# Groups of 768 tokens: twelve second products in hand, softmax transposes on 96 partitions in place, separate accounts for VectorE and ScalarE

## The chip, the cores and the metric

The kernel runs on one core of a Trainium2 chip. What counts is the device time of one execution in microseconds (us). TensorE does the matrix products, VectorE, ScalarE and GpSimd the elementwise work, and SyncE (SP) issues the DMAs. In rows of the trace the engines are PE (PEld for its weight loads), DVE, ACT, POOL and SP. Each engine runs its own instructions in order and waits on semaphores of the others.

## What is computed

```python
# 8 batches, 8 heads, 576 tokens, head size 64; heads 0-3 plain window of 32, heads 4-7 dilated by 4
scores = scale * q @ k^T, masked to the window
attn   = exp(scores - max) / (sum + 1e-9)
x      = (attn @ v), 8 heads side by side      # 4608 tokens x 512
h = x @ w_in                                   # 512 -> 2048
g = where(h > 0, h, exp(min(h, 0)) - 1)        # ELU
out = g @ w_out                                # 2048 -> 512
```

## The kernel before

**Split operands.** A 32-bit operand is kept as a high part and a rest, and a product is made of three: high by high, rest by high, high by rest. Making the parts is one ScalarE copy (a *cast*) and one VectorE subtraction (a *rest*) each.

**Chunks and groups.** The first 1536 tokens go through the two layers as three chunks of 512 (loop over `c` in `range(CS)`, line 913, 16 blocks `f` of 128 hidden columns each). The other 3072 tokens go as four groups of 768 (`superchunk`, line 773), each of two halves of 384 tokens. In a group the first layer is done by seven block products in place of eight: a *round* (`q`, 8 a group) makes two blocks of hidden columns for both halves, in seven *steps* (`s`, 0 to 6; `ORDER`, `MOVING`). A step is six matmuls of 128x384 (`product`, line 708; rows `h<-...`).

**A round's elementwise work** (`TODO`, line 54). The products accumulate in two PSUM tiles, x (steps 0, 1, 2, 5) and y (3, 4, 6). ScalarE copies x out after steps 0, 1 and 2 (`u1`, `u2`, `u3`; rows `e<-h`) and after step 5 (`C21`; row `a-1<-h`). VectorE adds y to one of the copies after steps 3, 4 and 6 (`C11`, `C22`, `C12`; rows `a-1<-h,e`). So step 1 waits for `u1`, step 2 for `u2`, step 4 for `C11`, step 6 for `C22`, and the next round's step 0 for `C21`. Then the ELU: `exp`, `relu` on ScalarE into one scratch tile `e` (rows `a<-...` 128x768), `elu` on VectorE. Block 1 (the odd one) comes from `C21` and `C22`, block 0 from `C11` and `C12`. A trailing `<` means the previous round's block. Last, `cast` and `rest` split the first half's 384 tokens into a *set* (`gh`, `gl`), and `keep` writes the second half's to DRAM (`aside`). After the eight rounds a loop over 16 blocks brings these back (`bring`), casts them and makes the operands of the next group (`OPERANDS`, `moving_operand`).

**Second products in hand.** A finished block is queued as three second products, one for each 128 tokens, of three 128x512 matmuls each (`push`, line 730; rows `o_ps<-...`). Step 5 queues block 1 and step 6 block 0, before their casts have run. `pop` takes products from the front of that queue (`fifo`), `POPS` says how many after each step: two after steps 0, 1 and 3. The first round uses `FIRST_POPS`. A finished output tile is copied by ScalarE and stored (`store`, line 608).

**Attention beside it.** Attention of later batches is done two heads' pairs at a time, in eight *blocks* (`BLOCKS`): an `S` piece (144 small score matmuls, then VectorE adds the masks), softmax steps held in a list (`side`), and an `O` piece (probabilities by values). `PIECES` gives the step (7q+s) at which a piece stands. `work(spare)` (line 443), called at `w0` to `w6`, takes softmax steps from the list as long as an account of VectorE time is positive; `work_all` empties it ahead of a piece. A block's two heads' pairs take turns in a fixed order. The probabilities are transposed by VectorE straight into the zeroed tiles `pt`, six 32-partition transposes for a pair (line 474). The chunk before the first group also makes blocks of batch 3 (`WHEN`), the first later block's scores (`EARLY`) and eight weight combinations (`COMBINE`).

The order on each engine in the groups is the program's own: `vec` and `act` (line 434) keep it.

Of the kernel before, what the change touches and what calls it, by code (L numbers as in the profile page):

```python
# [23 lines left out]
P = 128  # L24
# [36 lines left out]
WHEN = {1: (0, 6, 7, 13), 2: (0, 4, 5, 9)}  # L61
EARLY = 10
# [12 lines left out]
def body(ctx: ExitStack, tc: tile.TileContext, q, k, v, masks, w_in, w_out, out):  # L75
# [359 lines left out]
    side, held, credit = [], [], [0.0]  # L435

    def work_all():

        while side:
            side.pop(0)[1]()  # L440
        credit[0] = 0.0

    def work(spare):

        credit[0] = min(credit[0] + spare, 0.0) if not side else credit[0] + spare
        while side and credit[0] > 0:
            cost, step = side.pop(0)
            step()
            credit[0] -= cost

    def later_probabilities(b, hps, groups):
# [9 lines left out]
        def steps(j):  # L461

            sm, (mx, sums), tr = sms[j], small[j], trs[j]
            yield 0.9, lambda: vec.tensor_reduce(out=mx, in_=sm, op=ALU.max, axis=mybir.AxisListType.X)
            yield 0.9, lambda: vec.tensor_tensor(out=sm, in0=sm, in1=wide(mx), op=ALU.subtract)
            yield 0.0, lambda: act.activation(out=sm, in_=sm, func=AF.Exp, scale=0.125)
            yield 0.9, lambda: vec.tensor_reduce(out=sums, in_=sm, op=ALU.add, axis=mybir.AxisListType.X)
            yield 0.1, lambda: vec.tensor_scalar(out=sums, in0=sums, scalar1=1e-9, scalar2=None, op0=ALU.add)
            yield 0.1, lambda: vec.reciprocal(out=sums, in_=sums)
            yield 0.9, lambda: vec.tensor_tensor(out=sm, in0=sm, in1=wide(sums), op=ALU.mult)  # L470
# [137 lines left out]
    def store(c, t, o_ps):  # L608
        if c < CS:
# [57 lines left out]
    def more_sets():  # L667

        sets[1:1] = [tuple(fp.tile([P, TC], F32R, name=n, bufs=m)[:, :TH] for n, m in (("gh", 3), ("gl", 2))) for _ in range(2)]
        out_tiles.extend(fp.tile([P, DM], F32, name=n, bufs=m) for n, m in (("h", 2), ("h", 2), ("gh", 3)))  # L670
# [64 lines left out]
    def activation(what):  # L735
# [7 lines left out]
        if do == "exp":  # L743
# [12 lines left out]
    def piece(what):  # L756
# [16 lines left out]
    def superchunk(c):  # L773
        x_ps = y_ps = None
        for q in range(NQ):
            base = (c * NQ + q) * 7
            for s in range(7):
                load_combined(base + s + RING)
                if (c, q, s) == (0, 2, 0):
                    more_sets()  # L780
# [6 lines left out]
                for what in TODO[s]:  # L787
# [8 lines left out]
                    elif what[0] == "w":  # L796
                        work(SPARE[s])
# [19 lines left out]
        for f in range(NF):  # L817
# [11 lines left out]
            work(2.0)  # L829
# [83 lines left out]
    for c in range(CS):  # L913
# [14 lines left out]
        for f in range(NF):  # L928
# [53 lines left out]
            if c == CS - 1 and f >= EARLY:  # L982
                work(2.6)
# [80 lines left out]
```

## Time and profile before

| | us |
|---|---|
| median of 3 runs (1000.48 to 1004.38) | 1004.24 |
| the profiled execution, its own time | 1003.11 |
| its span, first to last instruction | 1001.3 |
| PE busy in it | 900.7 |
| DVE busy | 624.7 |
| ACT busy | 474.7 |

The first group begins at 347.26 us of the span, the next ones at 529.71, 686.84 and 847.29. A row of the timeline begins with start and length, and gives in brackets the engine's idle time ahead of it and what ended that.

### The profile page before, as it was taken

To read this page: it belongs to the slowest core of one execution; us is meant where nothing else is said; L and a number is where in the kernel's file an instruction comes from. 1 tells how busy PE (TensorE), PEld (TensorE's weight loads), DVE (VectorE), ACT (ScalarE), POOL (GpSimd) and SP (SyncE) were. 2 spreads that over 40 slices of the span, in tenths; PEclk is the share of its full clock that TensorE was granted. 3 is DMA by queue.
4 is the path that set the end of the run, shared out by engine and by line. 5 is a ranking of instruction groups with operands and counts; after the bars stand their busy time and mean duration, and the time that the engine had idled before them with its cause. 6 is when DMAs were issued, how large, how long until landed. Compare 5 with 4: busy or idle time off the path is not lost.

```text
span 1001.3 us, 17241 instructions
## 1 busy us (share of the span) xinstructions
PE 900.7 (90%) x6752; PEld 726.6 (73%) x6752; DVE 624.7 (62%) x1015; ACT 474.7 (47%) x913; POOL 6.0 (1%) x12
## 2 busy tenths in 40 slices
PE   6999999999898897897799888989788989888888
PEld 5446677788676676787687767878677878877766
DVE  6999989676886875747461857353566526233331
ACT  4765666465544543443453435453443444444442
POOL 2000000000000000000000000000000000000000
PEclk8999999999998997998999999999999989999999
DMA  9977352235444256755454765634754543655532
GB/s 352 382 260 248 98 159 94 81 125 200 167 156 142 56 157 186 222 166 175 124 159 150 213 191 169 192 114 121 223 161 144 175 127 87 200 167 167 157 103 79
DMA packets 93457, 166.45 MB, mean 166 GB/s; under 512 B 9696, under 2 KB 40768, under 8 KB 93376
## 3 DMA queue, kind: packets, MB, share of 16 engines
q1 hardware_dynamic: 93376, 165.36, 52.4%
q8 instruction: 53, 0.87, 0.4%
q14 instruction: 28, 0.23, 0.1%
HBM read 124.42 MB, written 40.89 MB: 165 GB/s over the span
## 4 chain that ended last, share of the span: by engine, by line
PE 59%; DVE 19%; ACT 15%; issue 4%; DMA 2%; SPq 0%; DVEq 0%; ACTq 0%
PE o_ps L112 31%; PE h L112 24%; ACT a L432 7%; DVE a-1_3348 L432 3%; PE a_ps L112 3%; DVE pt L419 2%; DVE pt L432 1%; ACT e L432 1%; DMA r<-combined 1%; DVE sums L432 1%; DVE a L432 1%; DVE r L432 1%; DVE e L584 1%; DMA out<-e 1%; ACT a-1_3348 L432 1%
## 5 line engine op out<-in xcount | busy, mean ns | idle before, releaser
L112 PE MATMUL h<-xall,r 128*128 128x384 f32 (+1 forms) x708 | 158.4, 371 | 5.7 <-DVE a-1_3348 L432 3.0
L112 PE MATMUL o_ps<-a,gh 128*128 128x512 f32 x434 | 149.3, 438 | 11.9 <-ACT gh L432 8.7
L112 PE MATMUL h<-r,r 128*128 128x384 f32 x526 | 130.5, 348 | 23.9 <-DVE a-1_3348 L432 16.2
L112 PEld LDWEIGHTS h<-xall,r 128*128 128x128 f32 x708 | 130.2, 192 | 24.7 <-DVE a-1_3348 L432 4.4
L112 PEld LDWEIGHTS h<-r,r 128*128 128x128 f32 x526 | 95.6, 193 | 35.4 <-DVE a-1_3348 L432 23.9
L112 PEld LDWEIGHTS o_ps<-a,gh 128*128 128x128 f32 x434 | 81.3, 190 | 45.0 <-issue 17.2
L432 DVE TENSOR_TENSOR a-1_3348<-h,e 128x384 f32<-128x384 f32 x96 | 53.2, 554 | 88.7 <-PE h L112 86.8
L432 ACT COPY e<-h 128x384 f32<-128x384 f32 x96 | 45.4, 473 | 128.1 <-PE h L112 126.9
L432 DVE SCALAR_TENSOR_TENSOR a-1_3348<-a-1_3348,a 128x768 f32<-128x768 f32 x64 | 61.2, 957 | 56.9 <-ACT a L432 50.6
L112 PE MATMUL h<-a,r 128*128 128x384 f32 x384 | 94.7, 340 | 0.0
L112 PE MATMUL o_ps<-r,gh 128*128 128x512 f32 x242 | 79.4, 410 | 9.6 <-ACT gh L432 8.8
L112 PE MATMUL o_ps<-a,r 128*128 128x512 f32 x288 | 77.5, 402 | 10.4 <-ACT r L432 7.5
L112 PE MATMUL o_ps<-a,gl 128*128 128x512 f32 x173 | 69.6, 402 | 6.1 <-DVE gl L588 3.7
L112 PEld LDWEIGHTS h<-a,r 128*128 128x128 f32 x384 | 70.6, 191 | 4.4
L112 PEld LDWEIGHTS o_ps<-a,r 128*128 128x128 f32 x288 | 53.1, 190 | 24.2 <-ACT r L432 9.1
L432 ACT COPY a-1_3348<-h 128x384 f32<-128x384 f32 x32 | 15.3, 479 | 110.2 <-PE h L112 106.5
L432 ACT ACTIVATE a<-a-1_3348 128x768 f32<-128x768 f32 x64 | 54.1, 846 | 21.6 <-DVE a-1_3348 L432 20.6
L432 ACT ACTIVATE a<-a 128x768 f32<-128x768 f32 (+1 forms) x72 | 60.4, 845 | 5.1 <-DVE a L432 3.2
L112 PEld LDWEIGHTS o_ps<-r,gh 128*128 128x128 f32 x242 | 46.6, 197 | 20.3 <-ACT gh L432 10.5
L432 DVE TENSOR_TENSOR r<-a-1_3348,r 128x384 fp32r<-128x384 f32 (+1 forms) x39 | 23.2, 596 | 45.9 <-ACT r L432 45.7
L112 PE MATMUL o_ps<-r,gl 128*128 128x512 f32 x117 | 48.0, 411 | 0.7 <-DVE gl L432 0.7
L112 PEld LDWEIGHTS o_ps<-a,gl 128*128 128x128 f32 x173 | 33.0, 191 | 16.4 <-DVE gl L588 5.0
(189 smaller groups left out, 1394.7 us busy)
## 6 DMA issues: line engine op xcount, KB each, us to landing
r<-combined SPq DMA_DIRECT2D x224, 256.0 KB, 3.0
aside<-a-1_3348 SPq DMA_DIRECT2D x64, 192.0 KB, 2.7
vt<-v SPq DMA_DIRECT2D x30, 384.0 KB, 3.9
kt<-k SPq DMA_DIRECT2D x30, 304.0 KB, 4.7
qt<-q SPq DMA_DIRECT2D x30, 288.0 KB, 4.2
r<-w_in SPq DMA_DIRECT2D x16, 512.0 KB, 7.1
r<-w_out SPq DMA_DIRECT2D x16, 512.0 KB, 7.8
combined<-a SPq DMA_DIRECT2D x20, 256.0 KB, 2.9
```

Source lines behind the costliest of these rows:

```text
L112: return inorder(nc.tensor.matmul(*args, **kw))
L419: last_transpose[b] = nc.vector.transpose(out=tr[ks, :, cs], in_=sm[cs, :, rs]).ins
L432: return lambda *args, **kw: inorder(getattr(self.eng, name)(*args, **kw))
L584: v.scalar_tensor_tensor(out=e, in0=h_ps, scalar=0.0, in1=e, op0=ALU.max, op1=ALU.subtract)
```

## The change

- The queue of second products is kept at twelve (an assertion at the end of each group says so): `FIRST_POPS` takes two fewer in the first round, and no piece stands any more at a step where it takes two beyond the table. Both casts and rests now stand at step 1.
- The odd block's ELU moves into its own round: its exponential is cut into two halves (`expR1` at step 4 from `C22`, `expL1` at step 5 from `C21`), `elu1` and `keep1` come after step 6.
- The probabilities are transposed in place by VectorE, two instructions on 96 partitions for a pair, and ScalarE copies six 32x384 pieces into `pt`.
- `work` has one account for VectorE and one for ScalarE, chooses the first step that is ready, and takes the two pairs of a block as they come. `work_all` empties the list only up to a given block.
- The pieces, the combinations, the attention of batch 3 and the first later block's scores move; one of the two extra sets and two output tiles come a round earlier; chunk 2's stores use them if they are there.

```diff
-FIRST_POPS = (2, 2, 1, 2, 1, 1, 1)
-TODO = [t.split() for t in ("u1 elu1< keep1< exp0< relu0< w0", "u2 elu0< keep0< cast1< rest1< w1", "u3 cast0< rest0< w2", "C11 w3", "C22 w4", "C21 exp1 relu1 w5 push1", "C12 w6 push0")]
-SPARE = (1.0, 0.6, 0.9, 1.5, 0.4, 1.3, 0.0)
+FIRST_POPS = (2, 2, 0, 2, 1, 1, 0)
+TODO = [t.split() for t in ("u1 exp0< relu0< w0", "u2 elu0< keep0< cast1< cast0< rest1< rest0< w1", "u3 w2", "C11 w3", "C22 expR1 w4", "C21 expL1 relu1 w5 push1", "C12 elu1 keep1 w6 push0")]
+SPARE = ((1.4, 0.4), (0.3, 0.9), (1.2, 1.7), (1.8, 1.7), (0.7, 0.0), (0.8, 0.0), (0.0, 0.0))
-WHEN = {1: (0, 6, 7, 13), 2: (0, 4, 5, 9)}
-EARLY = 10
+WHEN = {1: (0, 6, 7, 13), 2: (0, 6, 7, 12)}
+EARLY = 14
-PIECES = {0: {1: "S1", 7: "O0", 21: "S2", 24: "O1", 40: "S3", 44: "O2"}, 1: {8: "S4", 28: "S5", 33: "O4", 50: "O5"}, 2: {8: "S6", 28: "S7", 33: "O6", 50: "O7"}}
+PIECES = {0: {14: "S1", 17: "O0", 28: "S2", 31: "O1", 42: "S3", 45: "O2"}, 1: {7: "S4", 28: "S5", 31: "O4", 45: "O5"}, 2: {7: "S6", 28: "S7", 31: "O6", 45: "O7"}}
-COMBINE = {(1, 11): 0, (1, 13): 1, (1, 15): 2, (2, 1): 3, (2, 2): 4, (2, 4): 5, (2, 6): 6, (2, 8): 7}
+COMBINE = {(1, 11): 0, (1, 13): 1, (1, 15): 2, (2, 1): 3, (2, 4): 4, (2, 6): 5, (2, 9): 6, (2, 11): 7}
...
+    def next_step(vec_free, act_free):
+        seen = set()
+        for n, (block, pair, copies, on_act, cost, step) in enumerate(side):
+            when, where = latest.get((block, pair), (0, on_act))
+            ready = (block, pair) not in seen and (where == on_act or when < turn[0]) and not (copies and block - 1 in made)
+            seen.add((block, pair))
+            if ready and (act_free if on_act else vec_free) > 0:
+                return n
...
-            for c in range(GU):
-                for r in range(2):
-                    yield 0.57, lambda ks=ks, cs=cs, rs=rs: vec.transpose(out=tr[ks, :, cs], in_=sm[cs, :, rs])
+            for r in range(2):
+                part = sm[:, :, r * G:(r + 1) * G]
+                yield False, False, 0.57, lambda part=part: vec.transpose(out=part, in_=part)
+            for r in range(2):
+                for c in range(GU):
+                    yield True, True, 0.45, lambda ks=ks, cs=cs, rs=rs: act.copy(out=tr[ks, :, cs], in_=sm[cs, :, rs])
...
-                if (c, q, s) == (0, 2, 0):
-                    more_sets()
+                if (c, s) == (0, 0) and q in (1, 2):
+                    more_sets(q == 2)
...
-        if c < CS:
+        if not out_tiles:
             o = fp.tile([P, DM], F32, name="e")
...
-            work(2.0)
+            work(2.0, 0.9)
...
-            if c == CS - 1 and f >= EARLY:
-                work(2.6)
```

**A round of the last group, PE and ACT.** No attention is left here. Names: `h_7961` and `h_8100` are the PSUM tile x of the seventh round in the kernel before and in the changed one; the set is the right name in `o_ps<-weights,set`. PE before, from the end of step 1:

```order
L112 MATMUL h_7961<-r_1240,r_1073 128x384 x2
L112 MATMUL o_ps_7626<-a_2016,r_1209 128x512 x3
L112 MATMUL o_ps_7630<-a_2016,r_1209 128x512 x3
L112 MATMUL h_7961<-a_1576,r_871 128x384
L112 MATMUL h_7961<-a_1620,r_871 128x384
```

PE in the changed kernel, the same place:

```order
L112 MATMUL h_8100<-r_1240,r_1073 128x384 x2
L112 MATMUL o_ps_7763<-a_2016,xall 128x512 x3
L112 MATMUL o_ps_7740<-a_1815,gh 128x512 x2
L112 MATMUL o_ps_7740<-a_1815,gl 128x512
L112 MATMUL h_8100<-a_1576,r_1073 128x384
```

ACT before, from the end of the round ahead of it:

```order
L432 COPY a-1_3348<-h_7870 128x384
L432 ACTIVATE a_2132<-a-1_3348 128x768
L432 ACTIVATE a_2132<-a_2132 128x768
L432 COPY e<-h_7961 128x384
L432 ACTIVATE a_2132<-a-1_3348 128x768
L432 ACTIVATE a_2132<-a_2132 128x768
L432 COPY e<-h_7961 128x384
L432 CAST r_1209<-a-1_3348 128x384
L432 COPY e<-h_7961 128x384
L432 CAST gh<-a-1_3348 128x384
```

ACT in the changed kernel, the same place:

```order
L432 ACTIVATE a_2132<-a-1_3238 128x384
L432 COPY a-1_3238<-h_8008 128x384
L432 ACTIVATE a_2132<-a-1_3238 128x384
L432 ACTIVATE a_2132<-a_2132 128x768
L432 COPY e<-h_8100 128x384
L432 ACTIVATE a_2132<-a-1_3238 128x768
L432 ACTIVATE a_2132<-a_2132 128x768
L432 COPY e<-h_8100 128x384
L432 CAST r_1209<-a-1_3238 128x384
L432 CAST r_871<-a-1_3238 128x384
L432 COPY e<-h_8100 128x384
```

Before, the products after step 1 read `r_1209`, the set that ACT casts behind `u2` of the same round. In the changed kernel they read sets cast one round earlier (`xall`, `gh`), while ACT casts `r_1209` and `r_871`; half of the odd block's exponential stands ahead of `C21`.

**The round after an S piece in the second group, DVE.** `h_5311` and `h_5326` are its PSUM tile y (the three rows that read it are `C11`, `C22`, `C12`), `sm` and `a_2132` the two pairs' probabilities. Before:

```order
L432 TENSOR_TENSOR gl<-a-1_3348,gh 128x384
L432 TENSOR_SCALAR sums<-sums 96x12
L432 TENSOR_TENSOR a-1_3348<-h_5311,e 128x384
L432 RECIPROCAL sums<-sums 96x12
L432 TENSOR_TENSOR a_2132<-a_2132,sums 96x768
L432 STREAM_TRANSPOSE pt_80<-sm 32x12x32
L432 TENSOR_TENSOR a-1_3348<-h_5311,e 128x384
L432 STREAM_TRANSPOSE pt_80<-sm 32x12x32 x3
L432 TENSOR_TENSOR a-1_3348<-h_5311,e 128x384
```

In the changed kernel:

```order
L432 TENSOR_TENSOR gl<-a-1_3238,gh 128x384
L432 STREAM_TRANSPOSE sm<-sm 96x12x32
L432 TENSOR_REDUCE sums<-a_2132 96x12
L432 TENSOR_TENSOR a-1_3238<-h_5326,e 128x384
L432 TENSOR_SCALAR sums<-sums 96x12
L432 RECIPROCAL sums<-sums 96x12
L432 TENSOR_TENSOR a_2132<-a_2132,sums 96x768
L432 STREAM_TRANSPOSE a_2132<-a_2132 96x12x32
L432 TENSOR_TENSOR a-1_3238<-h_5326,e 128x384
L432 STREAM_TRANSPOSE a_2132<-a_2132 96x12x32
L432 TENSOR_TENSOR a-1_3238<-h_5326,e 128x384
```

The transposes write the probabilities' own tiles, four in all for the block instead of twelve; more softmax work stands between `C11` and `C22`.

**The second round of the first group, ACT.** `o_ps_2619` to `o_ps_2631` are chunk 2's four output tiles, `h_3669` and `h_3554` the round's tile x. Before:

```order
L303 COPY x_3717<-a_ps_3691 128x12x4x8
L618 COPY e<-o_ps_2619 128x512
L618 COPY e<-o_ps_2623 128x512
L432 COPY e<-h_3669 128x384
L432 CAST xall<-a-1_3348 128x384
L618 COPY e<-o_ps_2627 128x512
L618 COPY e<-o_ps_2631 128x512
L432 COPY e<-h_3669 128x384
```

In the changed kernel:

```order
L432 CAST xall<-a-1_3238 128x384
L645 COPY h<-o_ps_2619 128x512
L432 CAST r_1209<-a-1_3238 128x384
L432 COPY pt_80<-sm 32x12x32 x2
L645 COPY h<-o_ps_2623 128x512
L432 COPY e<-h_3554 128x384
L432 COPY pt_80<-sm 32x12x32 x3
L432 ACTIVATE a_2132<-a_2132 96x768
L645 COPY h<-o_ps_2627 128x512
L645 COPY h<-o_ps_2631 128x512
L432 ACTIVATE a_2132<-a-1_3238 128x384
```

The stores stand later in the round and go through two tiles `h` in turn, instead of the four tiles `e` that `u1` to `u3` use too.

More of the change, by code (lines that the diff above doesn't have):

```diff
@@ L434, in body, with run, work, work_all @@
     vec, act = Ordered(nc.vector), Ordered(nc.scalar)
[L435 to L449, printed above, removed]
+    side, credit, turn, latest = [], [0.0], [0], {}
+    def run(n):
+        block, pair, copies, on_act, cost, step = side.pop(n)
+        step()
+        latest[block, pair] = turn[0], on_act
+        return on_act, cost
+    def next_step(vec_free, act_free):
[6 more added lines that the diff above has]
+                return n
+        return None
+    def work(vec_spare, act_spare):
+        turn[0] += 1
+        credit[0] += vec_spare
+        while True:
+            n = next_step(credit[0], act_spare)
+            if n is None:
+                break
+            on_act, cost = run(n)
+            if on_act:
+                act_spare -= cost
+            else:
+                credit[0] -= cost
+        credit[0] = min(credit[0], 0.0)
+    def work_all(block):
+        turn[0] += 1
+        while side and side[0][0] <= block:
+            run(0)
     def later_probabilities(b, hps, groups):
@@ L469, in steps @@
-            yield 0.1, lambda: vec.reciprocal(out=sums, in_=sums)
-            yield 0.9, lambda: vec.tensor_tensor(out=sm, in0=sm, in1=wide(sums), op=ALU.mult)
-            for c in range(GU):
-                for r in range(2):
+            yield False, False, 0.9, lambda: vec.tensor_reduce(out=mx, in_=sm, op=ALU.max, axis=mybir.AxisListType.X)
+            yield False, False, 0.9, lambda: vec.tensor_tensor(out=sm, in0=sm, in1=wide(mx), op=ALU.subtract)
+            yield False, True, 0.85, lambda: act.activation(out=sm, in_=sm, func=AF.Exp, scale=0.125)
@@ new lines, in steps @@
+            yield False, False, 0.9, lambda: vec.tensor_reduce(out=sums, in_=sm, op=ALU.add, axis=mybir.AxisListType.X)
+            yield False, False, 0.15, lambda: vec.tensor_scalar(out=sums, in0=sums, scalar1=1e-9, scalar2=None, op0=ALU.add)
+            yield False, False, 0.2, lambda: vec.reciprocal(out=sums, in_=sums)
+            yield False, False, 0.9, lambda: vec.tensor_tensor(out=sm, in0=sm, in1=wide(sums), op=ALU.mult)
+            for r in range(2):
+                part = sm[:, :, r * G:(r + 1) * G]
+                yield False, False, 0.57, lambda part=part: vec.transpose(out=part, in_=part)
@@ L479, in later_probabilities @@
+        block = BLOCKS.index((b, hps[0]))
+        side.extend((block, j, *step) for j in range(2) for step in steps(j))
         return [(b, hp, tr) for hp, tr in zip(hps, trs)]
@@ L665, in body, with more_sets @@
     sets, rows, ring, arrivals, out_tiles = [], [], [], [], []
-    def more_sets():
-        sets[1:1] = [tuple(fp.tile([P, TC], F32R, name=n, bufs=m)[:, :TH] for n, m in (("gh", 3), ("gl", 2))) for _ in range(2)]
-        out_tiles.extend(fp.tile([P, DM], F32, name=n, bufs=m) for n, m in (("h", 2), ("h", 2), ("gh", 3)))
+    def more_sets(last):
+        sets.insert(1, tuple(fp.tile([P, TC], F32R, name=n, bufs=m)[:, :TH] for n, m in (("gh", 3), ("gl", 2))))
+        out_tiles.extend(fp.tile([P, DM], F32, name=n, bufs=m) for n, m in ((("gh", 3),) if last else (("h", 2), ("h", 2))))
     def flat(name, a, b):
@@ L742, in activation @@
         gh, gl = group[2][1 - odd]
-        if do == "exp":
+        if do in ("expL", "expR"):
+            half = int(do == "expR")
+            act.activation(out=e[:, half, :], in_=h[:, half, :], func=AF.Exp)
+        elif do == "exp":
             act.activation(out=e, in_=h, func=AF.Exp)
@@ L759, in piece @@
         b, hp = BLOCKS[i]
-        work_all()
+        work_all(i - (what[0] == "S"))
         if what[0] == "S":
@@ L764, in piece @@
             outputs_piece(made.pop(i))
-            side.extend(held)
-            held.clear()
     def bring(f):
@@ L796, in superchunk @@
                     elif what[0] == "w":
-                        work(SPARE[s])
+                        work(*SPARE[s])
                     elif what[0] == "p":
```

9 lines of the change are left out of this document (1 added, 8 removed).

## The prediction

> **What bounds the kernel now.** I read the busy times first, then the four groups by windows, then PE's waits there, and last one round of the last group along the chain of waits.
>
> ```profile
> PE 900.7 (90%) x6752; PEld 726.6 (73%) x6752; DVE 624.7 (62%) x1015; ACT 474.7 (47%) x913; POOL 6.0 (1%) x12
> ...
> 347.26:529.71 182.45, 159.71 (x1267) 136.91 (x1267) 113.45 (x193) 77.63 (x141) 0.00 (x0) 0.92 0.54 163
> 529.71:686.84 157.13, 140.38 (x1009) 119.03 (x1008) 87.11 (x143) 69.70 (x123) 0.00 (x0) 0.99 0.57 170
> 686.84:847.29 160.45, 143.24 (x1010) 121.42 (x1008) 87.59 (x149) 69.94 (x125) 0.00 (x0) 0.97 0.51 154
> 847.29:1001.30 154.01, 136.24 (x649) 116.19 (x647) 46.07 (x73) 60.06 (x105) 0.00 (x0) 0.98 0.48 144
> ```
>
> PE is busy for 90% of the span, and in the groups (length, then busy PE, PEld, DVE, ACT, POOL, then PE's clock) neither DVE nor ACT is busy for two thirds of the time. Who holds PE up between 347 and 1001 us:
>
> ```profile
> PE h L112 <- DVE a-1_3348 L432: 20.1, 13, 6.4
> PE o_ps L112 <- ACT gh L432: 17.5, 10, 3.0
> PE o_ps L112 <- ACT r L432: 13.6, 10, 3.0
> PE o_ps L112 <- ACT xall L432: 8.1, 5, 3.0
> PE o_ps L112 <- DVE r L432: 3.3, 3, 1.5
> PE h L112 <- ACT h L432: 3.2, 1, 3.2
> PE o_ps L112 <- DVE gl L432: 3.1, 4, 1.5
> PE h L112 <- DMA r<-combined: 2.3, 2, 1.5
> PE h L112 <- ACT e L432: 2.2, 1, 2.2
> PE o_ps L112 <- DVE xall L432: 0.6, 1, 0.6
> ```
>
> The `o_ps` rows are second products waiting for their own cast or rest: 17.5 + 13.6 + 8.1 + 3.3 + 3.1 + 0.6 = 46.2 us in 33 waits. The `h` rows are first products: 27.8 us in 17 waits. A wait costs more than its idle time, as a round shows:
>
> ```profile
> 891.89 1.88 PE o_ps L112 x6
> 893.77 2.11 PE h L112 x12
> 895.87 1.39 PE o_ps L112 x6
> 897.26 2.17 PE h L112 x12
> ...
> 899.46 0.49 ACT a-1_3348 L432
> ...
> 904.44 0.37 ACT e L432
> 904.81 0.42 ACT r L432
> ```
>
> ```profile
> 905.27 1.87 PE L112 MATMUL o_ps<-a,r 128*128 128x512 f32 x6 [1.33 <-ACT r L432]
> ```
>
> The next such product starts at 905.27 (timeline), so the round takes 905.27 - 891.89 = 13.38 us. Its work is 42 first-product matmuls, 12 in 2.10, and 18 of the second product, six in 1.39: 7.35 + 4.17 = 11.52. So 1.86 us are lost, where the timeline has 1.33 of idle time. The rest, 0.53, is the pipeline filling again (the six take 1.87, not 1.39 apart). With it the second products lose 46.2 + 33 x 0.53 = **63.7 us** and the first ones 27.8 + 17 x 0.53 = **36.8**. The chain names the cause: `C21` on ACT at 899.46, both ELUs, `u2` at 904.44, the cast at 904.81, and the product behind step 1 waits for that cast. Only eight products are in hand by then: the six queued in the last round and two older ones, which step 0 takes.
>
> Longer waits also halve PE's clock:
>
> ```profile
> 958.39 0.73 PE L112 MATMUL o_ps<-r,gh 128*128 128x512 f32 x2 [3.04 <-ACT gh L432]
> ...
> 960.04 1.05 PE L112 MATMUL o_ps<-r,gh 128*128 128x512 f32 x2
> ...
> 963.25 0.62 PE L112 MATMUL o_ps<-r,gh 128*128 128x512 f32 x2
> ```
>
> After 3.04 us of idle time two matmuls take 1.05, later 0.62. From the windows' clock, 0.08 x 182 + 0.01 x 157 + 0.03 x 160 + 0.02 x 154 = 24 us are lost to it, part of it while PE was idle anyway; I count half, **12**. All together 112 us are lost in the groups. The Trainium skill, "TensorE: Matmul & The Clock Gate" (What's actually happening), has the clock fall after an idle window of about 3.4 us; here 3.04 us were enough, and by its rule this term would be smaller, an estimate of 8.
>
> **The change, part by part.**
>
> *Twelve in hand.* The queue starts at 14 (four blocks of four, two popped); the first round now takes 8 and adds 6, and no score piece takes two extra. With twelve, a round pops what was queued two rounds ago, and its cast ran a whole round (11.5 us) before. The 33 waits go. What is late next is a group's end: six products (4.2 us) now stand ahead of the last casts instead of two (1.39), and there the wait was 3.04; I leave 0.5 at each of four ends. Remaining: 2 of 63.7, so **-61.7**. The sets suffice: five, two a round, and each is rewritten two rounds after its last product is popped.
>
> *The odd block's ELU and the two halves.* ACT's work per round stays within 0.1 us: two halves in place of one 0.846. But `expR1` now stands ahead of `C21` and waits for `C22`. Behind it on ACT: `C21`, and behind that PE's next step 0. DVE starts `C22` 0.2 after step 4, takes 0.55, then the half exponential about 0.47: 1.2 us, against step 5's 1.04 plus 0.2, so `C21` starts on time while DVE is free, with 0.3 to spare behind it. `keep1` moves ahead on SP by one place: SP waits for `elu1`, about 2 us after step 6, and behind it stands the weight load of the next round's step 4, due 8 us later and landing in 3.0.
>
> ```profile
> L432 DVE TENSOR_TENSOR a-1_3348<-h,e 128x384 f32<-128x384 f32 x96 | 53.2, 554 | 88.7 <-PE h L112 86.8
> L432 ACT ACTIVATE a<-a-1_3348 128x768 f32<-128x768 f32 x64 | 54.1, 846 | 21.6 <-DVE a-1_3348 L432 20.6
> L432 DVE STREAM_TRANSPOSE pt<-a 32x384 f32<-32x384 f32 x48 | 27.3, 568 | 0.9
> L369 ACT COPY pt<-c 64x192 f32<-64x192 f32 (+1 forms) x16 | 5.0, 312 | 0.4
> L432 DVE TENSOR_REDUCE nmx<-a 96x12 f32<-96x768 f32 x8 | 7.5, 940 | 0.0
> L432 DVE SCALAR_TENSOR_TENSOR a-1_3348<-a-1_3348,a 128x768 f32<-128x768 f32 x64 | 61.2, 957 | 56.9 <-ACT a L432 50.6
> r<-combined SPq DMA_DIRECT2D x224, 256.0 KB, 3.0
> ```
>
> *Transposes.* A block loses twelve of 0.568 (6.8 us of DVE) and gains four on 96 partitions. No row has that: bounds 0.568 and three times that, 1.70. I take 0.57, since DVE's 96- and 128-partition rows (0.940, 0.957) show that time doesn't go with partitions: 2.3, so DVE has 4.5 less a block. The Trainium skill, "VectorE: DVE Perf Modes" (The three transpose paths), has the transposer work on separate 32x32 blocks, so that one instruction would do three at once; no run here shows it. ACT gains twelve copies of 32x384 a block: between 0.312 (192 elements) and 0.568 (DVE's own); I take 0.43, 5.2 us a block, where ACT is busy for 70 of 157 us.
>
> *Rounds with softmax steps.* Here DVE sets the pace:
>
> ```profile
> 591.44 0.75 DVE L432 TENSOR_TENSOR a<-o_ps,masks_sb 96x256 f32<-96x256 f32 x2 [2.32 <-PE o_ps L112]
> 592.11 0.47 DVE L432 TENSOR_TENSOR a<-a_ps,masks_sb 96x128 f32<-96x128 f32 x2
> 592.51 1.01 DVE L432 TENSOR_TENSOR sm<-a_ps,masks_sb 96x384 f32<-96x384 f32 x2
> ...
> 503.03 1.80 PE a_ps L112 x40
> ```
>
> After an S piece come masks 2.0, `elu0` 0.96, two rests of 0.55, two steps of 0.94 and `C11` 0.55: 6.5 us, 6.8 with 0.15 for a semaphore at each end. PE asks for `C11` after three steps (1.05 each) and four pops (2 x 1.39): 5.9. That is 0.9 late, and `C22` behind two more steps of 0.94 is another 0.4. In five of the seven blocks made in the groups an O piece stands between steps 3 and 4 of that round (1.80 us for 40 of its 48 matmuls) and covers it. In the round after, `C22` stands behind two small steps, a product and a transpose (about 1.9 together) and `u2` behind a softmax exponential (96x768, taken as the 0.846 above): 1.1 us. With refill I take 2.0 for two rounds, 0.5 for five, and 1.5 for the seven after: 17 us (bounds: 0, if every step finds a gap; 40, if each of these 14 rounds keeps its `C11` wait and one more of 1.3).
>
> *The first group's start and chunk 2.*
>
> ```profile
> 305.46 0.80 PE L112 MATMUL o_ps<-a,gl 128*128 128x512 f32 x1 [3.34 <-DVE gl L588]
> ...
> 386.52 2.29 PE L112 MATMUL h<-r,r 128*128 128x384 f32 x6 [6.35 <-DVE a-1_3348 L432]
> ```
>
> ```profile
> 381.04 0.58 ACT L618 COPY e<-o_ps 128x512 f32<-128x512 f32 x1 [4.71 <-DMA out<-e]
> ```
>
> The longest wait, 6.35, comes from ACT holding for chunk 2's stores at 381.04. The new stores go out later, through two tiles `h`; the third waits until the first has landed, and `expR1` and `C21` stand behind it. I take 2.5 of the 6.9. At the very start (the waits of 3.2 and 2.2 for ACT) 12 transposes leave DVE and the score masks come in; `u1` still waits behind the last cast of chunk 2: 6.0 of 6.5 stay. So first products keep 17 + 8.5 + 3.4 (the two DMA waits with refill, taken as unchanged) = 29 of 36.8: **-8**. With the long waits gone (6.35, four of about 3 at the ends) the clock keeps 4 of 12: **-8**. Chunk 2 itself loses the softmax steps that made waits such as the one at 305.46, but its values piece now stands where DVE is busiest: between -7 (that wait, 1.08 ahead of it, and the slow clock after) and +4 (softmax 17 us, two combinations 6.6 and five ELUs 6.9 against 27 us of PE); I take 0.
>
> **Sum.** 61.7 + 8 + 8 = 77.7 off the profiled execution's 1003.1 (span 1001.3; the median shown is 1.1 above it): **925.4 us**.
>
> **Rivals.**
>
> *Half the gain.* With no product waits, PE asks 1.9 us sooner each round. `u2` was at 904.44 and ended at 904.81. Without the wait PE ends step 1 at 891.89 + 11.52 + 0.34 of refill = 903.75 and two pops later, at 905.1, wants `u2` done. So about 0.3 us are spare, 0.6 with the shorter exponential ahead, and side copies in front of `u2` eat them. If every round of three groups loses 1 us and the 14 softmax rounds another 1: 38 us, **963**. For it: the chain through the one scratch tile `e` is as long as ever. Against: copies are kept to steps 1 to 3 by ACT's own account.
>
> *Slower.* The same chain, place `expR1`: if it, and `C21` behind it, came later than reckoned by x us in all 32 rounds, PE would lose x - 0.3 + 0.53 in each. It decides from x = 2.2, where 32 x 2.43 = 78 us are given back; at 2.6 the time is 925.4 + 32 x 2.83 = **1016**. Only DVE steps of over 2 us ahead of `C22` in every round could do that, and the last group has none.
>
> *It doesn't do what it says.* If sets or output tiles held the casts back, products would wait as before: **1000**. Against: the count of sets above.
>
> *All hidden.* Softmax rounds and chunk 2 at their lower bounds: 925.4 - 17 - 7 = **901**.
>
> **How the numbers follow.** The forecast (905 to 945) has 0.67, half the gain (945 to 985) 0.17, all hidden 0.10, without effect 0.03, slower 0.03. The range 901 to 968 takes in the forecast, most of all hidden (0.05) and two thirds of half the gain. A measurement of this kernel can tell about 0.5% from no change: faster by that 0.94, within it 0.03, slower 0.03.
>
> **What would show it.** Right: no `o_ps` wait of over 0.6 us in the rounds, a round of 11.5 us in the last group, transposes of 0.57 on 96 partitions, and what is left of waits as `h <- DVE` in softmax rounds. Wrong: transposes near 1.7, `h` waits for ACT's `C21` or `u2` in rounds without softmax, or the clock at a half more often than now.

## The result, and the profile after

The changed kernel takes **904.06 us** (median of four runs, 903.81 to 905.21), the kernel before 1004.31 (1000.48 to 1006.14): a ratio of 0.9008, interval [0.8981, 0.9036]. The forecast was 925.4 with a range of 901 to 968. The profiled execution has a span of 902.2 us against 1001.3.

The page's busy times, and then the four groups by windows (the stretch and its length, then busy PE, PEld, DVE, ACT, POOL, PE's clock, DMA share, GB/s), both of the changed kernel:

```profile
PE 868.0 (96%) x6752; PEld 714.3 (79%) x6752; DVE 586.2 (65%) x951; ACT 529.5 (59%) x1041; POOL 6.0 (1%) x12
```

```profile
332.35:489.02 156.67, 147.71 (x1256) 126.16 (x1255) 105.83 (x180) 104.05 (x199) 0.00 (x0) 0.99 0.62 191
489.02:627.08 138.06, 135.51 (x1010) 119.00 (x1009) 77.93 (x127) 83.01 (x155) 0.00 (x0) 1.00 0.64 193
627.08:764.58 137.50, 135.44 (x1010) 118.95 (x1009) 78.43 (x133) 83.20 (x157) 0.00 (x0) 1.00 0.59 180
764.58:902.20 137.62, 133.52 (x661) 118.76 (x659) 46.02 (x73) 62.61 (x113) 0.00 (x0) 1.00 0.53 161
```

PE is busy for 96% of the span instead of 90, and from the second group on at full clock. Against the windows of before:

| stage | before, us | after, us | change | forecast |
|---|---|---|---|---|
| ahead of the first group | 347.26 | 332.35 | -14.9 | 0 (between -7 and +4) |
| group 1 | 182.45 | 156.67 | -25.8 | |
| group 2 | 157.13 | 138.06 | -19.1 | |
| group 3 | 160.45 | 137.50 | -22.9 | |
| group 4 | 154.01 | 137.62 | -16.4 | |
| the four groups | 654.04 | 569.85 | -84.2 | -77.7 |

Two thirds of the error stand ahead of the groups. With twelve in hand the first group also takes four second products fewer than before (8 instead of 10 and S3's two), which the last group finishes: 4 x 3 matmuls of 0.2315 us, so 2.8 us of the first group's change only move to the last. Who holds PE up within them (the changed kernel's waits of PE between 332 and 902 us: total, times, longest):

```profile
PE h L112 <- DVE a-1_3238 L432: 3.7, 4, 2.3
PE h L112 <- ACT e L432: 2.7, 3, 2.2
PE o_ps L112 <- ACT nothing L523: 2.0, 1, 2.0
PE h L112 <- DMA r<-combined: 1.2, 3, 0.5
PE h L112 <- ACT a-1_3238 L432: 1.1, 1, 1.1
PE a_ps L112 <- ACT pt L432: 0.8, 2, 0.4
PE h L112 <- DVE sums L432: 0.7, 1, 0.7
PE o_ps L112 <- DVE gl L432: 0.7, 2, 0.3
PE o_ps L112 <- DVE xall L432: 0.3, 1, 0.3
PE o_ps L112 <- DVE r L432: 0.3, 1, 0.3
```

The second products' waits, 46.2 us in 33 before, are now the last three rows: 1.3 us in four, one at each group's end. (`o_ps <- ACT nothing` is not one of them: there a scores piece waits for `nothing`, a small ScalarE copy out of one of its banks that stands as a marker in that engine's queue.) A round of the last group, by PE's timeline from the products behind its step 3 (24 first-product matmuls, four steps, follow until the next ones) to the same ones a round later:

```profile
840.58 0.63 PE L112 MATMUL o_ps<-a,gh 128*128 128x512 f32 x2
...
852.04 1.55 PE L112 MATMUL o_ps<-a,r 128*128 128x512 f32 x6
```

852.04 - 840.58 = 11.46 us, the 11.5 that the prediction worked out for a round without a wait.

The new instructions, from the groups by line and shape (count, then busy time and mean ns of one):

```profile
L432 ACT ACTIVATE a<-a-1_3238 128x384 f32<-128x384 f32 x64 | 33.6, 525 | 69.2 <-DVE a-1_3238 L432 68.1
L432 ACT COPY pt<-sm 32x384 f32<-32x384 f32 x48 | 24.5, 510 | 0.5
L432 DVE STREAM_TRANSPOSE sm<-sm 96x384 f32<-96x384 f32 x16 | 9.0, 569 | 0.3
```

A transpose on 96 partitions takes 0.569 us, as one on 32 did. A copy of probabilities takes 0.51 (0.43 was taken), a half exponential 0.525 (0.47).

### The profile page after: what moved, and what is told of

It reads as the page before. It is cut to its first block, busy times and chain, and to the rows that moved or that the text cites. A ratio compares the mean times of both kernels' runs of the same rounds, so it can differ in the third digit from the quotient of the medians.

```text
span 902.2 us, 17335 instructions
## 1 busy us (share of the span) xinstructions
PE 868.0 (96%) x6752; PEld 714.3 (79%) x6752; DVE 586.2 (65%) x951; ACT 529.5 (59%) x1041; POOL 6.0 (1%) x12
## 4 chain that ended last, share of the span: by engine, by line
PE 63%; DVE 18%; ACT 13%; issue 3%; DMA 3%; SPq 0%; DVEq 0%; ACTq 0%
PE o_ps L112 32%; PE h L112 27%; ACT a L432 6%; PE a_ps L112 3%; DVE a-1_3238 L432 3%; ACT pt L432 2%; DVE pt L419 2%; DMA r<-combined 1%; DVE a L432 1%; DVE a L157 1%; DVE a L155 1%; DVE sums L432 1%; DMA out<-h 1%; DVE r L432 1%; ACT a-1_3238 L432 1%
## 5 line engine op out<-in xcount | busy, mean ns | idle before, releaser
L112 PE MATMUL h<-xall,r 128*128 128x384 f32 (+1 forms) x708 | 154.3, 365 | 4.9 <-DVE a-1_3238 L432 2.3
L112 PEld LDWEIGHTS h<-xall,r 128*128 128x128 f32 x708 | 127.0, 188 | 23.3 <-DVE a-1_3238 L432 4.7
L112 PE MATMUL h<-r,r 128*128 128x384 f32 x526 | 127.1, 341 | 5.7 <-ACT e L432 2.2
L432 DVE TENSOR_TENSOR a-1_3238<-h,e 128x384 f32<-128x384 f32 x96 | 53.0, 552 | 112.8 <-PE h L112 112.2
L432 ACT ACTIVATE a<-a-1_3238 128x384 f32<-128x384 f32 (+1 forms) x96 | 60.7, 632 | 83.5 <-DVE a-1_3238 L432 82.5
L432 DVE SCALAR_TENSOR_TENSOR a-1_3238<-a-1_3238,a 128x768 f32<-128x768 f32 x64 | 61.2, 956 | 49.2 <-ACT a L432 49.2
L112 PE MATMUL o_ps<-r,gh 128*128 128x512 f32 x242 | 75.6, 393 | 0.7 <-ACT e L645 0.6
L432 ACT COPY e<-h 128x384 f32<-128x384 f32 x96 | 45.7, 476 | 49.1 <-PE h L112 46.0
L112 PE MATMUL o_ps<-a,r 128*128 128x512 f32 x288 | 72.4, 392 | 0.0
L432 ACT ACTIVATE a<-a 128x768 f32<-128x768 f32 (+1 forms) x72 | 60.2, 845 | 1.9
L112 PE MATMUL o_ps<-r,gl 128*128 128x512 f32 x117 | 46.0, 393 | 0.7 <-DVE gl L432 0.7
L419 DVE STREAM_TRANSPOSE pt<-sm 32x384 f32<-32x384 f32 x72 | 40.9, 568 | 0.9
L112 PE MATMUL o_ps<-a,xall 128*128 128x512 f32 x153 | 39.7, 394 | 0.0
L601 ACT ACTIVATE e<-h 128x512 f32<-128x512 f32 x44 | 27.1, 618 | 20.0 <-PE h L112 19.4
```

The source lines that it names most:

```text
L112: return inorder(nc.tensor.matmul(*args, **kw))
L419: last_transpose[b] = nc.vector.transpose(out=tr[ks, :, cs], in_=sm[cs, :, rs]).ins
L432: return lambda *args, **kw: inorder(getattr(self.eng, name)(*args, **kw))
L601: a.activation(out=e, in_=h_ps, func=AF.Exp)
```

## The experiments

"More" and "less" are against the changed kernel's 904.06 unless another is named; lengths of stages are between the first products of each group in the profiled runs. Each run stood beside runs of the kernel before, whose median was between 1003.75 and 1004.93 us.

### Twelve in hand, undone alone

```diff
-FIRST_POPS = (2, 2, 0, 2, 1, 1, 0)
+FIRST_POPS = (2, 2, 2, 2, 2, 1, 1)
```

> The changed kernel with only eight second products in hand (the first round takes twelve instead of eight; nothing else is altered). Theory A, the twelve in hand cover the last steps of a round and of a group: the product waits of before come back, 46.2 us idle and 0.53 of refill for each of 33 = 63.7 us, with half of the clock's 24 us in the groups: 55 to 75 us more than the changed kernel, 959 to 979 us, with two waits or more at each of the four group ends again. Theory B, the own accounts and the shorter transposes made the rounds even, and the products in hand matter little: at most 20 us more, up to 924 us.

Measured: **984.04 us** (982.53 to 985.56), ratio to before 0.9801 [0.9771, 0.9831]: 80 more. PE's waits in that run's groups, the three largest rows and all those of first products:

```profile
PE o_ps L112 <- ACT r L432: 21.0, 13, 2.8
PE o_ps L112 <- ACT gh L432: 17.9, 11, 2.8
PE o_ps L112 <- ACT xall L432: 12.3, 8, 2.8
...
PE h L112 <- ACT e L432: 2.2, 1, 2.2
PE h L112 <- DVE a-1_3238 L432: 1.0, 1, 1.0
```

The product waits are back, 51.2 us in 32 for ACT's casts alone, and theory B falls. It is more than the 75 of theory A, and the stages say where: groups 2 to 4 take 153.5, 155.5 and 150.6 us, some 4 less than before each, but the first takes 189.5, 7 more than before. The kernel before had ten in hand there until its piece S3 took two; this run has eight from the first round on.

### Twelve in hand alone, on the kernel before

```diff
-FIRST_POPS = (2, 2, 1, 2, 1, 1, 1)
+FIRST_POPS = (2, 2, 0, 2, 1, 1, 0)
-PIECES = {0: {..., 40: "S3", 44: "O2"}, ...
+PIECES = {0: {..., 42: "S3", 45: "O2"}, ...
...
+        sets.insert(1, ...)
```

> The kernel before with only the twelve in hand (the first round takes eight, piece S3 of the first group two steps later so that it takes nothing from them, working sets and store tiles as in the changed kernel); chunk 2, the ELU order, the transposes and the one account stay as before. Theory A: 55 to 75 us less than the kernel before, 929 to 949 us, so that this part and chunk 2 (15 us) make up nearly the whole change. Theory B, the accounts and transposes are needed for it: at most 30 us less, 974 us or more, because the softmax steps of the old account still make the combinations late in the rounds after a scores piece.

Measured: **939.19 us** (936.45 to 942.24), ratio 0.9364 [0.9328, 0.9401]: 65 less than before. Theory A holds for the size; with chunk 2's 15 us it makes 80 of the 100, not nearly the whole. With the run above this makes a square: the twelve give 65 us alone and 80 on top of the rest; the rest gives 20 alone and 35 on top of the twelve. But that run is not the kernel before with the rest added, since it has eight in the first group where the kernel before has ten. The lengths of the other groups, where both have eight, are a clean square:

| group, us | before | the rest alone | the twelve alone | both |
|---|---|---|---|---|
| 2 | 157.1 | 153.5 | 143.3 | 138.1 |
| 3 | 160.5 | 155.5 | 143.2 | 137.5 |
| 4 | 154.0 | 150.6 | 138.2 | 137.6 |
| together | 471.6 | 459.6 | 424.6 | 413.2 |

Here the two parts simply add: 12.0 and 47.0 alone, 58.4 together. That the twelve look worth more on top of the rest comes from the first group. The waits say the same. With eight in hand the rest takes the first products' 27.8 us in 17 waits down to the 3.2 in two shown above, and the second products' waits for ACT's casts grow from 17.5 + 13.6 + 8.1 = 39.2 us in 25 to 51.2 in 32; of these 12.0 us the first group has 10.9 (5.4 us in 3 before, 16.3 in 8 in that run).

### Ten in hand

```diff
-FIRST_POPS = (2, 2, 0, 2, 1, 1, 0)
+FIRST_POPS = (2, 2, 1, 2, 1, 1, 1)
```

> The changed kernel with ten second products in hand (the first round takes ten). Two more in hand than in the run with eight cover 2 x 3 x 0.2315 = 1.39 us more of each round's end. Theory A, each wait is simply shortened by that cover: the plain rounds' waits (1.07 us with eight) go, the rounds with a pair, the rounds after a piece and the group ends (1.4 to 3.3 us with eight) keep the rest: about 15 us idle and 10 us of refill of the 63 that the run with eight shows, 920 to 930 us. Theory B, every product in hand is worth the same: half of the 80 us between eight and twelve, about 944 us. Theory C, ten are enough: within 5 us of the changed kernel, up to 909 us.

Measured: **918.00 us** (915.17 to 919.12), ratio 0.9138 [0.9114, 0.9162]. Eight, ten and twelve give 984, 918 and 904: the first two are worth 66, the next two 14. That is theory A, a little under its 920 to 930, and the rounds show it: no second product waits within a round of groups 2 to 4, and each of the four ends keeps one wait of 1.4 us for ACT and one of 0.3 for DVE.

```profile
PE o_ps L112 <- ACT gh L432: 2.8, 2, 1.4
...
PE o_ps L112 <- ACT xall L432: 1.4, 1, 1.4
PE o_ps L112 <- ACT r L432: 1.4, 1, 1.4
```

With eight the ACT wait at such an end was 2.77 (the rows of 2.8 above), and 2.77 - 1.39 = 1.38: a wait shortens by just the product time put ahead of it, and with twelve nothing is left of it. These four waits, some 8 us with refill, are only a part of the 14. The first group is 6.9 us longer than with twelve, 1.4 of them for the two products that it takes more; its longest wait for a combination is 4.0 us instead of 2.3, and the waits for weights (`h <- DMA`) are 3.9 instead of 1.2 over all groups. Why, is not shown.

### The accounts

The changed kernel with the softmax steps of before (their transposes and the fixed order of the two pairs), `TODO` of before (the ELU order, and block 0's cast and rest at step 2), and `work` and `work_all` as before:

```diff
-                    work(*SPARE[s])
+                    work(SPARE[s])
...
-SPARE = ((1.4, 0.4), (0.3, 0.9), (1.2, 1.7), (1.8, 1.7), (0.7, 0.0), (0.8, 0.0), (0.0, 0.0))
+SPARE = (1.0, 0.6, 0.9, 1.5, 0.4, 1.3, 0.0)
```

> The changed kernel with the softmax steps of before: one account that covers both engines in listed order, the two pairs of a block interleaved, twelve 32-partition transposes on VectorE, the ELU order of before; twelve in hand, chunk 2 and the places of the pieces stay as in the changed kernel. The transposes of before alone gave -2 us and the ELU order alone +2, so what this run shows above 904 us is the accounts. Theory A, they matter even with twelve in hand: the twelve alone on the kernel before left 35 us to the changed kernel, of which chunk 2 is 8.7, so 20 to 28 us more, 924 to 932 us, lost as waits of first products for VectorE's combinations in the softmax rounds. Theory B, the remainder was the pieces' old places and the accounts hardly matter: within 8 us, up to 912 us.

Measured: **931.34 us** (930.78 to 932.47), ratio 0.9271 [0.9249, 0.9293]: 27 more, theory A. The first row of PE's waits in the groups of that run, and one such wait, by DVE's and by PE's timeline:

```profile
PE h L112 <- DVE a-1_3238 L432: 23.9, 16, 3.4
```

```profile
568.98 0.94 DVE L432 TENSOR_REDUCE sums<-a 96x12 f32<-96x768 f32 x1
569.96 0.17 DVE L432 TENSOR_SCALAR sums<-sums 96x12 f32<-96x12 f32 x1
570.16 0.22 DVE L432 RECIPROCAL sums<-sums 96x12 f32<-96x12 f32 x1
570.42 0.95 DVE L432 TENSOR_TENSOR a<-a,sums 96x768 f32<-96x768 f32 x1
571.29 0.55 DVE L432 TENSOR_TENSOR a-1_3238<-h,e 128x384 f32<-128x384 f32 x1
```

```profile
571.89 1.45 PE L112 MATMUL h<-xall,r 128*128 128x384 f32 x6 [2.98 <-DVE a-1_3238 L432]
573.14 2.12 PE L112 MATMUL h<-r,r 128*128 128x384 f32 x6
```

Four softmax steps in a row (2.3 us) stand ahead of the combination at 571.29, and more ahead of them; PE waits 2.98 us for it, and the second six matmuls behind it run at half clock (2.12 us). Nine of the 16 waits (18.1 us) have such steps right ahead of the combination, seven (5.8 us) the 32-partition transposes. The changed kernel has four such waits, 3.7 us, in place of 16. The next run has the same transposes with two accounts, and this one takes 29.6 us more than it; the ELU order alone, with two accounts, is worth 2. So some 27 us go with the accounts, the second part of the change. No run tells apart what came with them: the account itself, the choice of the first ready step, the order of the pairs and `work_all`. Block 0's cast and rest at step 2 are in the 27 us too.

### Transposes and ELU order, each undone alone

```diff
-                yield False, False, 0.57, lambda part=part: vec.transpose(out=part, in_=part)
...
-                    yield True, True, 0.45, lambda ...: act.copy(out=tr[ks, :, cs], in_=sm[cs, :, rs])
+                    yield True, False, 0.57, lambda ...: vec.transpose(out=tr[ks, :, cs], in_=sm[cs, :, rs])
```

> The changed kernel with the transposes of before (six of 32 partitions to a pair straight into the tile of probabilities, no copies on ScalarE, held while the block ahead still has its output piece to come). Theory A, VectorE is off the path (65 % busy) and the twelve in hand take what it does more: within 4 us of the changed kernel, 900 to 908 us. Theory B, VectorE's time in the softmax rounds sets the first products: eight blocks, each with 12 x 0.57 - 4 x 0.57 = 4.6 us more on VectorE, of which half shows: 10 to 25 us more, 914 to 929 us.

Measured: **901.72 us** (900.44 to 901.87), ratio 0.8978 [0.8953, 0.9004], an interval that overlaps the changed kernel's: theory A. But the total hides two effects. By windows of that run:

```profile
332.30:482.00 149.70, 145.00 (x1255) 125.15 (x1254) 124.55 (x212) 80.31 (x151) 0.00 (x0) 1.00 0.65 201
482.00:622.00 140.00, 136.63 (x1010) 118.81 (x1010) 87.51 (x143) 71.55 (x131) 0.00 (x0) 1.00 0.63 191
622.00:761.90 139.90, 136.44 (x1010) 118.69 (x1009) 87.92 (x149) 71.53 (x133) 0.00 (x0) 1.00 0.59 177
```

Undone, the transposes make the first group 7.0 us shorter and the second and third 1.9 and 2.4 longer. The busy shares would not have told this: undone, VectorE is busy for 124.55 of 149.70 us in the first group and for 87.51 of 140.00 in the second, yet it is the first that gets shorter. What PE waits for there is ScalarE's order, in which copies of block 0's probabilities stand ahead of the marker `nothing` of S1 (the changed kernel's row, then this run's, in which no copy stands ahead of it):

```profile
371.14 0.15 ACT L523 COPY nothing<-o_ps 96x1 f32<-96x1 f32 x1
```

```profile
363.22 0.15 ACT L520 COPY nothing<-o_ps 96x1 f32<-96x1 f32 x1 [0.16 <-PE o_ps L112]
```

PE's waits of 2.34, 1.06 and 2.05 us between 361 and 372 us shrink to one of 1.27 in this run. Undone for block 0 alone (a run further down), the transposes make the first group 3.9 us shorter, so that this block has more than half of the 7.0.

```diff
-TODO: "... exp0< relu0< w0", ..., "C22 expR1 w4", "C21 expL1 relu1 w5 push1", "C12 elu1 keep1 w6 push0"
+TODO: "... elu1< keep1< exp0< relu0< w0", ..., "C22 w4", "C21 exp1 relu1 w5 push1", "C12 w6 push0"
```

> The changed kernel with the exponential of the odd row in one piece at step 5 and its last sum and store in the round after, as before (the even row's casts stay at step 1). Theory A, with twelve in hand the ELU order is covered: within 2 us, 902 to 906 us. Theory B, the half exponential ahead of C21 is needed to have rows' buffers free for the next round's combinations: 16 rounds with C11 or C22 late by 0.5 us or more in the softmax rounds, 8 us or more above, 912 us or later.

Measured: **906.38 us** (905.26 to 908.33), ratio 0.9024 [0.9003, 0.9045]: 2 more, within what can be told from nothing. Theory B falls. Block 0's casts stay at step 1 here.

### Chunk 2

```diff
-EARLY = 14
+EARLY = 10
...
+            if c == CS - 1 and f >= EARLY:
+                work(2.6, 0.9)
```

and `WHEN` and `COMBINE` as in the kernel before.

> The changed kernel with chunk 2 as before (scores piece S0 at row 10 and its softmax steps in rows 10 to 15, the attention pieces at rows 4, 5 and 9, the combinations at their old rows). Theory A, the gain ahead of the first group came from chunk 2: 13 to 17 us more than the changed kernel, 917 to 921 us, all of it ahead of the first group. Theory B, the gain there came from elsewhere (the twelve in hand reach back into the first group, or the two profiles differ by chance): within 4 us, 900 to 908 us.

Measured: **912.80 us** (911.81 to 913.56), ratio 0.9091 [0.9065, 0.9117]: 9 more. Both theories miss the total, but the stages fit A: the first group starts at 346.7 us, 14.4 later, and then takes 150.3 instead of 156.7; block 0's softmax steps, in chunk 2 here, are done by then. So chunk 2's gain of 14.4 is partly a debt that the first group pays, as the next run confirms.

Only the rows of pieces and combinations back (`WHEN` and `COMBINE`), with `EARLY` still 14:

> The changed kernel with chunk 2's attention pieces (rows 4, 5, 9) and weight combinations (rows 2, 4, 6, 8) back in their old rows, but with scores piece S0 still at row 14 and no softmax steps in chunk 2. Undoing both put the first group 14.4 us later. Theory A, the spacing gives it: the waits from 273 to 306 us of before (2.07, 0.43, 1.08 and 3.33 us idle) stand before row 10, so they come back and the waits from 338 to 347 us don't: first group 8 to 11 us later than in the changed kernel, 912 to 915 us. Theory B, softmax steps leaving chunk 2 gives it: first group at most 3 us later, up to 907 us.

Measured: **913.81 us** (912.34 to 916.31), ratio 0.9098 [0.9072, 0.9124]; the first group starts at 344.3, 12 later. Theory A, the spacing, and 12 where 8 to 11 were expected. PE's waits between 240 and 344 us of that run, first two rows:

```profile
PE o_ps L112 <- DVE gl L615: 3.7, 2, 3.3
PE o_ps L112 <- ACT gh L614: 3.1, 2, 2.1
```

The changed kernel has 0.7 us in each of these two (one wait each). Both rows are products that wait for a row's own cast or rest; with the combinations and pieces spread over more rows, these come in time. Which of the two spreads does it is not told apart. The first group takes 155.5 us here, 5.3 more than in the run before this one, which differs by S0's row and its softmax steps in chunk 2. At the old spacing, taking these steps out of chunk 2 thus gains 2.4 us ahead of the group (344.3 against 346.7) and costs 5.3 in it.

### What is left in the first group

Three edits to its 156.7 us. First the store that ScalarE waits for:

```profile
362.25 0.59 ACT L645 COPY h<-o_ps 128x512 f32<-128x512 f32 x1 [3.44 <-DMA out<-h]
```

```diff
-        if not out_tiles:
+        if not out_tiles or (c, t) == (CS - 1, 2):
```

> The changed kernel with the third of chunk 2's four stores out of a tile e instead of h, so that the fourth need not wait for the landing of an earlier one. Theory A, the 3.44 us that ScalarE waits there makes the exponentials, C21 and the copies of the probabilities late in the first group (TensorE's waits of 2.34, 1.06 and 2.05 us from 361 to 372 us): 3 to 6 us less than the changed kernel, 898 to 901 us. Theory B, the ScalarE work queued there (twelve copies of a block among it) is late by itself: within 1.5 us, 902.5 to 905.5 us.

Measured: **904.48 us** (903.44 to 907.65), ratio 0.9013 [0.8988, 0.9037]: nothing. ScalarE's wait is gone from that run, but PE's is not: by DVE's, PE's and ScalarE's timelines of it

```profile
357.99 0.95 DVE L432 TENSOR_REDUCE sums<-a 96x12 f32<-96x768 f32 x1 [2.29 <-ACT a L432]
...
360.31 0.55 DVE L432 TENSOR_TENSOR a-1_3238<-h,e 128x384 f32<-128x384 f32 x1
```

```profile
360.91 1.34 PE L112 MATMUL h<-xall,r 128*128 128x384 f32 x6 [2.33 <-DVE a-1_3238 L432]
```

```profile
365.87 3.09 ACT L432 COPY pt<-a 32x384 f32<-32x384 f32 x6
368.98 0.15 ACT L523 COPY nothing<-o_ps 96x1 f32<-96x1 f32 x1
```

VectorE's sum waits for block 0's second exponential on ScalarE, the combination stands behind the sum, and six copies stand ahead of the marker `nothing` that the piece S1 waits for. Right ahead of that exponential ScalarE's timeline has three more copies (1.56 us). The store's wait lay beside these.

Second, the group's pieces a round later:

```diff
-PIECES = {0: {14: "S1", 17: "O0", 28: "S2", 31: "O1", 42: "S3", 45: "O2"}, ...
+PIECES = {0: {21: "S1", 24: "O0", 35: "S2", 38: "O1", 49: "S3", 52: "O2"}, ...
```

> The changed kernel with the first group's pieces a round later (S1 at the start of round 3 instead of round 2, O0, S2, O1, S3, O2 each seven steps later too). Theory A, the waits of 2.34, 1.06 and 2.05 us from 361 to 372 us come from block 0's steps, which S1 forces onto both engines before round 2, six copies of 0.51 us ahead of ScalarE's marker for S1 among them: they go with their refill, 4 to 7 us less than the changed kernel, 897 to 900 us. Theory B, the start of the first group has too much other work on both engines (operands, first stores), whenever S1 comes: within 2 us, 902 to 906 us.

Measured: **910.60 us** (909.04 to 911.29), ratio 0.9062 [0.9035, 0.9089]: 6.5 more, a miss on the other side of both theories. The wait for `nothing` went, the 2.34 for VectorE stayed, and a new one came at the group's end, where O3 now follows S3 too closely (ScalarE's, then PE's timeline):

```profile
463.45 3.11 ACT L432 COPY pt<-a 32x384 f32<-32x384 f32 x6
```

```profile
463.48 2.19 PE L112 MATMUL a_ps<-pt,vt 128*64 128x96 f32 x24 [3.98 <-ACT pt L432]
...
468.73 4.21 PE L112 MATMUL o_ps<-r,r 128*128 128x512 f32 x9
```

The copies of that block come just ahead of its output piece; PE waits 3.98 us and the nine matmuls behind the piece take 4.21 us at half clock, 2.20 elsewhere.

Third, the transposes of before for block 0 alone:

> The changed kernel with the transposes of before for the first block of the first group alone (twelve transposes on VectorE straight into the probabilities, no copies on ScalarE); all later blocks transpose in place on 96 partitions. The run with the transposes of before throughout took 7 us less in the first group and 1.9 and 2.4 more in the second and third. Theory A, the copies of that first block cost ScalarE's queue there and the in-place transposes pay elsewhere: 5 to 8 us less than the changed kernel, 896 to 899 us. Theory B, the 7 us came from the group's other three blocks: within 2 us of the changed kernel.

Measured: **899.11 us** (898.83 to 899.42), ratio 0.8954 [0.8934, 0.8974]: 5 less, at the small end of theory A. The first group takes 152.8 and the two after it what they took.

Last, a version that beats both kernels: the transposes of before for the first group's four blocks, and its last operands moved out of the way of chunk 2's last ELU.

```diff
-NEXT = "cast:B21 rest:B21 make:T4 cast:T1 rest:T1".split()
-FIRST = [... "cast:T4 rest:T4", "cast:B22 rest:B22", "", "", "", "", ""]
+NEXT = []
+FIRST = [... "cast:B21 rest:B21 make:T4", "cast:T1 rest:T1", "cast:T4 rest:T4", "cast:B22 rest:B22", "", "", ""]
```

> The changed kernel with two edits in its first group: the transposes of before for all four blocks of that group (the in-place ones from the second group on), and the last moving operands of that group (B21, T4, T1 and the rest) made step by step within its first round instead of ahead of the last ELU of chunk 2. Theory A, the stages add: the first group as in the run with the transposes of before (149.7 instead of 156.7 us), the later ones as in the changed kernel (138 each), and the wait of 2.23 us at 337 us gone with its refill, because the last ELU is no longer behind five operand steps on VectorE: 7 to 10 us less than the changed kernel, 894 to 897 us. Theory B, the operands come late for their products instead, or the softmax steps of the second group pay for the first's: 897 to 902 us.

Measured: **896.22 us** (894.65 to 898.19), ratio 0.8922 [0.8902, 0.8942]: 8 less, theory A. The windows of that run's first two groups:

```profile
335.00:483.30 148.30, 144.89 (x1255) 125.11 (x1254) 124.16 (x212) 81.71 (x154) 0.00 (x0) 1.00 0.64 203
483.30:620.80 137.50, 135.46 (x1010) 118.94 (x1009) 78.10 (x127) 83.19 (x155) 0.00 (x0) 1.00 0.63 194
```

The first group is 8.4 shorter than in the changed kernel, and the wait at 337 us is gone (one of 1.4 came eight us later). It begins 2.7 later and ends at 483.3, where the run with the transposes of before throughout, whose first group has the same transposes, ends it at 482.0. So no gain of the operands' new place is shown; the gain is that of the transposes, now without their cost of 2 us in each of the next two groups.

## Why the prediction was right, and where it was not

**Twelve in hand: right in kind and size.** Forecast -61.7. From the two waits views the idle time fell by 46.2 - 1.3 = 44.9 us and 29 waits, with 0.53 of refill each 60.3; alone on the kernel before it measured -65, with the clock's share, which the prediction counts apart (in that run's groups 2 to 4 the clock is 1.00). The group ends were put at 0.5 us of waiting; they have 0.3.

**Chunk 2: mis-sized, and outside its bounds.** The term was 0, between -7 and +4; it measured -14.9 at the first group's start. The step that failed: it read the wait of 3.34 us as the doing of the softmax steps that leave chunk 2, and the later piece and spread combinations as a cost. The run with the old rows has that wait (3.3) without any of those steps, and shows that the spacing itself gives 12 of the 14.4. The trace of before could have told: its wait stands at 305.46 us, behind six transposes of chunk 2's own attention (L419, 300.60 to 304.07), and the first of the steps in question (L432) begins at 319.83. What the prediction also lacked is the debt: steps that leave chunk 2 arrive in group 1, and cost 5 to 6 us there.

**Rounds with softmax steps: mis-sized.** First products were to keep 29 of 36.8 us. The five `h` rows after sum to 9.4 us in 12 waits, 15.8 with refill: -21 where -8 was forecast. Seven rounds after a block were each to lose 1.5; PE's waits in such a round (517.6 to 530 us) have no row at all. The step that failed is that the sum has no term for the two accounts, as if they changed an order and no time; undone, they measure some 27 us with what came with them. Against that stand waits that the prediction did not have: 2.0 us for `nothing` and 0.8 for copies of probabilities, 4.4 with three refills. The 0.15 us allowed for a semaphore at each end is too much: the traces have, in the median of such waits, 0.04 from PE's matmul to VectorE and 0.055 back.

**Clock.** It was to keep 4 of 12. By the windows it loses 0.01 x 157 = 1.6 of 24, so by the same half -11 instead of -8. With these the groups' sum is -60.3 - 21 + 4.4 - 11 = -88, where -84.2 was measured: 0.53 for each wait and half of the clock together count some 4 us too much, and which of them does is not shown.

**Stores and the group's start.** A wait for a store came, at the fourth store instead of the third (3.44 us on ScalarE). The forecast had 2.5 us of it reach PE, and PE does wait 2.34 at that place; but the run without the store's wait keeps 2.33 of it, because VectorE's combination stands behind the softmax sum there. So the number is near by luck, and the cause was another. Of the two waits at the very start, 6.0 us of which were to stay, only one of 2.2 did.

**The rivals.** Half the gain needed `expR1` and the side copies to delay `C21` and `u2` in plain rounds: in groups 2 and 3, where the copies are made, no first product waits for ACT at all, and in the first group, behind its start, three do (1.06, 0.24 and 0.24 us). The slower rival needed `C22` late by 2.2 us in all rounds; the ELU order turned out to be worth 2 us in all. The 904.06 lies within the range, but just under the forecast's own band (905 to 945, chance 0.67) and 3 us over "all hidden" (901, chance 0.10). That rival had the softmax rounds and chunk 2 at their lower bounds, which is where both came out, chunk 2 beyond it.

## What to carry to other kernels

A queue of finished work ahead of a late producer pays by the time that it covers: measure the wait, divide by the time of one item, and stop there (two more took 66 us, the next two 14). Once that wait is gone, the next one needs its own cure; where the comparison is clean, in groups 2 to 4, the two gains just add (47 and 12 alone, 58 together). Whether it pays to move work to a less busy engine is settled in the stage where it lands, by what it stands ahead of there and not by busy shares: the same copies cost 7 us in the first group, and the shorter transposes gained 2 in each of the next two.

## What the runs showed of the hardware

The transpose in place on 96 partitions takes no longer than one on 32 (0.569 against 0.568 us for 384 elements): three blocks for the price of one. ScalarE's copy of 32x384 takes 0.510 us, as its cast of 128x384 does (0.512): there too no price of the partitions shows.

PE's clock can fall after less than the 3.04 us shown in the prediction, and not each time. In the run with eight in hand each of the four groups ends with the same wait of 2.77 us (its timeline of PE):

```profile
484.87 4.06 PE L112 MATMUL o_ps<-r,xall 128*128 128x512 f32 x9 [2.77 <-ACT xall L432]
...
643.03 0.73 PE L112 MATMUL o_ps<-r 128*128 128x512 f32 x2 [2.77 <-ACT r L432]
...
796.26 1.22 PE L112 MATMUL o_ps<-r,gh 128*128 128x512 f32 x2 [2.77 <-ACT gh L432]
...
938.39 0.77 PE L112 MATMUL o_ps<-r,gh 128*128 128x512 f32 x2 [2.77 <-ACT gh L432]
...
940.04 1.05 PE L112 MATMUL o_ps<-r,gh 128*128 128x512 f32 x2
```

After the first and the third the matmuls are slow at once (nine in 4.06 us instead of 2.20, two in 1.22 instead of 0.63), after the fourth only a microsecond later, and after the second two take 0.73. The clock granted in the 3 to 4 us behind each is 0.56, 1.00, 0.50 and 0.57. What decides between them was not tried.
